# First layer of a two-layer network: the 64 left-over rows of its contraction as one full product of stacked high and low weights and two 64-row products on the two halves of the array

## The chip, the core and the metric

The kernel runs on one core of a Trainium2 chip. The metric is the device time of one execution in microseconds (us); the time before is the median of three runs. TensorE (PE) multiplies, VectorE (DVE) and ScalarE (ACT) read its results from the accumulator memory, GpSimd (POOL) works on ordinary memory only, and SyncE (SP) issues all transfers.

## The reference

```
S, D, DFF = 2048, 576, 4608
h  = x + irfft2(rfft2(layernorm(x)) * (w_r + i w_i))      # x: 2048 x 576
h2 = h + relu(layernorm(h) @ w1) @ w2                     # w1: 576 x 4608, w2: 4608 x 576
```

All of it is float32. The kernel keeps that precision in the two layers on products that take rounded inputs (type fp32r): each operand v is split into a high part (v rounded) and a low part (v minus the high part), and a product a·b becomes high·high + high·low + low·high, three products in place of one.

## The kernel before, in words

The work has four stages: the forward transform, a spectral stage (`mid_d`, `mid_b`, `mid_i`), the inverse transform mixed with the first units of the network, and the long part in which only the network is left, from about 225 us on.

**The units.** The hidden width of 4608 is cut into 18 groups of 256 (two halves of 128, index `a`), the 2048 tokens into 4 chunks of 512. A group with a chunk is a unit, 72 in all, in the order of the list `steps` (L685, L686). The first layer of a unit is `mm1` (L460 to L481): for each half, products of 512 columns that accumulate into one bank. The contraction over 576 is four full blocks of 128 rows and 64 left-over rows. Each full block takes three products (high weights with high tokens, high with low, low with high). For the left-over rows the tokens are stacked: block 4 of the token buffer `xc` holds the low part in partitions 0 to 63 and the high part in 64 to 127, and the high and low weights of block 4 stand twice, in both halves of the partitions. So one full product with the high weights gives high·low + high·high, and one with the low weights gives the rest (L470). That is 14 products a half and 28 a unit.

**The second layer.** The first 8 units multiply hidden values by `w2` in `mm2`. From unit 8 on (`WINO`), `slot` (L626) does it with seven products of half-size blocks, each of them six instructions of 288 columns (`prod`, L562), 42 a unit, whose results VectorE adds to the output (`add`, L569). The order is written out by hand: `quarter(k)` puts a quarter of the next unit's first layer between the products of this one, half `a = k // 2`, and the instructions whose number over 7 equals `k % 2`. The products of this unit and of the next share TensorE in that order, in two accumulators of the second layer (`wps[0]`, `wps[1]`) and two of the first (`wps[2]`, `wps[3]`, one for each half, used in turn by even and odd units).

**The weights.** `load_weights` loads a group's weights; the 64 left-over rows of `w1` are loaded twice, into both halves of the partitions (L300, L301). `split_weights` allots the high and low copies (five blocks of 256 columns) and lists the pieces. `split` (L305) makes the high part on ScalarE and the low part on VectorE (L307). From group 3 on `slot` does one piece at a time.

**The tokens.** In the inverse stage, `norm2` normalises two token tiles of 128 on ScalarE (`ln_apply`, L222), one at the end of each step of the loop at L689. `project` (L442 to L455) transposes a tile on TensorE in five blocks: four of columns 0 to 511 (L446) and a fifth of columns 448 to 575 (L447), which puts the left-over columns into partitions 64 to 127. ScalarE writes the high parts of all five blocks (L451) and a copy (L453), GpSimd subtracts for the low parts of the four full blocks (L454), VectorE for the left-over ones (L455, on 64 partitions). The token buffer has 9 blocks: 5 high ones and 4 low ones. At step 17 of the loop `project` comes before the products of the network (L703), otherwise behind them.

**Shapes of products.** In the spectral stage the products have 64 output rows; pairs of them go to output partitions 0 to 63 and 64 to 127 of the same bank (L336 to L341). All other products are full, 128 by 128. Float32 inputs make two instructions of a product, fp32r inputs one. `warm_pe` (L276) runs products of the identity that nobody reads; two calls (L386, L388) stand at the end of the spectral stage, behind 64-row outputs.

Of the kernel before, what the change touches and what calls it, by code (L numbers as in the profile page):

```python
# [11 lines left out]
F32R = mybir.dt.float32r  # L12
# [4 lines left out]
S, D, DFF = 2048, 576, 4608  # L17
# [110 lines left out]
def kernel(ctx: ExitStack, tc: tile.TileContext, x, w_r, w_i, w1, w2, cc2, c1, fb, ib, c3, out):  # L128
    nc = tc.nc
# [3 lines left out]
    def sb(shape, tag, bufs=1, dt=F32):  # L133
        n[0] += 1
        return pool.tile(shape, dt, tag=tag, name=f"{tag}_{n[0]}", bufs=bufs)

    n = [0]

    def ps():
        n[0] += 1  # L140
        return psum.tile([128, 1024], F32, tag="d", name=f"d_{n[0]}", bufs=4)

    def ebuf(shape, dt=F32):
        e = sb([128, EW], "e", EB, dt)[:, :int(np.prod(shape[1:]))]
        return e.rearrange("p (a b) -> p a b", a=shape[1]) if len(shape) == 3 else e

    def mm(o, l, r, start, stop):
        nc.tensor.matmul(o, l, r, start=start, stop=stop)  # L148

    def act(o, i, **kw):  # L150
        nc.scalar.activation(o, i, AF.Copy, **kw)  # L151

    xs = sb([128, NT, D], "X")
# [7 lines left out]
    ident = sb([128, 128], "ident")  # L161
# [55 lines left out]
    def ln_apply(xs, t0, k, mvr, zs):  # L217

        r = mvr[2]
        for i in range(k):  # L220
            yield
            nc.scalar.activation(zs[i], xs[:, t0 + i, :], AF.Identity, bias=r[:, 2, i:i + 1], scale=r[:, 1, i:i + 1])  # L222
# [6 lines left out]
    stats, zin = {}, {}  # L229
# [64 lines left out]
    raw, wts = {}, {}  # L294
# [9 lines left out]

    def split(h, l, v):  # L305
        act(h, v)
        nc.vector.tensor_sub(l, v, h)  # L307

    pieces = []

    def work(k):
        for _ in range(k):
            split(*pieces.pop(0))

    def split_weights(g, part):
        if g == 1 and part == 0:
            h, l = tail[0][:, 4608:5888], tail[0][:, 5888:7168]
        else:
            h, l = (ebuf([128, (1280, 1152)[part]], F32R) for _ in range(2))
        h, l = (v.rearrange("p (a n) -> p a n", a=(5, 2)[part]) for v in (h, l))  # L320
        wts[g, part] = h, l
        for k in range((5, 2)[part]) if g >= 2 else [slice(None)]:
            pieces.append((h[:, k], l[:, k], raw[g][part][:, k]))
        if g <= 2:
            work(len(pieces))

    tail = []
# [61 lines left out]
    xs = sb([128, NT, D], "A")  # L389
# [2 lines left out]

    dev = c3t[:, :580].rearrange("p (a n) -> p a n", a=4)
    lpv = c3t[:, 580:].rearrange("p (a n) -> p a n", a=2)
    xc01 = sb([128, 2, 9, 512], "B", dt=F32R)
    xc2 = sb([128, 9, 512], "C", dt=F32R)
    xc = [xc01[:, 0], xc01[:, 1], xc2]
    Es = {}

    def inv_d(t):  # L400
        pd = ps()
        ut = [dims(U, 64 * (32 * b + 2 * t), [1, 128]) for b in range(5)]
        for r in range(2):
            o = pd[:, 512 * r:512 * r + 290]
            mm(o, ut[4], lpv[:, r], True, False)
            for h in range(2):
                mm(o[:, 145 * h:145 * h + 145], ut[2 * ((r + h) % 2) + r], dev[:, 2 * r + h], False, h == 1)
        ez = ebuf([128, 578 + D])
        pdv = pd.rearrange("p (r n) -> p r n", r=2)
        e0, e1 = ez[:, :289], ez[:, 289:578]  # L410
        R2 = [289, 2]
        pa_, pb_ = pdv[:, :, 0:145], pdv[:, :, 145:290]
        ea = dims(ez, 0, R2, [1, 145])
        act(ea, pa_)
        nc.vector.tensor_sub(dims(ez, 288, R2, [-1, 144]), ea[:, :, :144], pb_[:, :, :144])  # L415
        nc.vector.tensor_add(ea, ea, pb_)  # L416
        y = ez[:, 578:]
        nc.gpsimd.tensor_sub(dims(ez, 578 + 575, [-1, 287]), e0[:, 1:288], e1[:, 1:288])
        nc.vector.tensor_add(y[:, 0:289], e0, e1)  # L419
        Es[t] = y  # L420
# [11 lines left out]
    def stat2(t):  # L432
        t0 = t - t % 2
        stats[t0] = ln_stats(xs, t0, 2, t % 2, stats.get(t0))

    def norm2(t0, k):
        z = ebuf([128, 2, D])
        for i in range(k):
            Zs[t0 + i] = z[:, i, :]
        return ln_apply(xs, t0, k, stats.pop(t0), [z[:, i, :] for i in range(k)])  # L440

    def project(t):  # L442
        y = Zs.pop(t)
        pz = ps()
        for b in range(4):
            nc.tensor.transpose(pz[:, 128 * b:128 * b + 128], y[:, 128 * b:128 * b + 128], ident)  # L446
        nc.tensor.transpose(pz[:, 512:640], y[:, 448:576], ident)  # L447
        q = slice(128 * (t % CH), 128 * (t % CH) + 128)
        dst = xc[t // CH]
        pzv = pz.rearrange("p (a s) -> p a s", s=128)  # L450
        act(dst[:, 0:5, q], pzv[:, :5])  # L451
        zt = ebuf([128, 512])
        act(zt, pz[:, :512])  # L453
        nc.gpsimd.tensor_sub(dst[:, 5:9, q], zt.rearrange("p (a s) -> p a s", s=128), dst[:, 0:4, q])  # L454
        nc.vector.tensor_sub(dst[0:64, 4, q], pzv[64:128, 4], dst[64:128, 4, q])  # L455

    hid = {}
    pend = {}

    def mm1(i, a, part=None):  # L460
        g, c = steps[i]
        w1h, w1l = wts[g, 0]
        if a == 0 and not part:
            pend[i] = None if i >= WINO else ps()
        p = hid_p(i, a) if i >= WINO else pend[i][:, 512 * a:512 * a + 512]
        f = slice(128 * a, 128 * a + 128)
        ops = []
        for kt in range(4):
            ops += [(w1h, kt, kt), (w1h, kt, 5 + kt), (w1l, kt, kt)]
        ops += [(w1h, 4, 4), (w1l, 4, 4)]  # L470
        for n_, (w, kt, xk) in enumerate(ops):
            if part is None or n_ // 7 == part:
                mm(p, w[:, kt, f], xc[c][:, xk, :], n_ == 0, n_ == len(ops) - 1)
        if i >= WINO:
            return
        if a == GF - 1:
            p = pend.pop(i).rearrange("p (a s) -> p a s", a=GF)
            hh, hl = sb([128, GF, 512], "D", 4, F32R), sb([128, GF, 512], "D", 4, F32R)
            nc.scalar.activation(hh, p, AF.Relu)
            nc.vector.scalar_tensor_tensor(hl, p, 0.0, hh, op0=ALU.max, op1=ALU.subtract)  # L480
            hid[i] = (hh, hl)  # L481
# [21 lines left out]
    WINO = 8  # L503
    wps, fs = [], {}
    NAMES = ("B22", "T4", "B11", "B21", "T2", "T1", "T3")

    def wform(n):
        o = 6208 + 576 * NAMES.index(n)
        return tail[0][:, o:o + 288], tail[0][:, o + 288:o + 576]

    def wino_sums(g, *ns):
# [9 lines left out]
    def wino_w(*names):  # L521
        for n in names:
            split(*wform(n), fs[n])

    def wino_tiles():
        D1, D2, D3 = (sb([128, 4, 256], "D", 4, F32R) for _ in range(3))
        E1, E2 = ebuf([128, 4, 256]), ebuf([128, 4, 256])
        hs = tail[0][:, 5184:5696], tail[0][:, 5696:6208]
        fs.update(p0=E1[:, 0:2], p1=E1[:, 2:4], S1=E2[:, 0], S2=E2[:, 1], S3=E2[:, 2], S4=E2[:, 3], S12=E2[:, 0:2])
        fs.update(A11=(D1[:, 0], D1[:, 1]), A12=(D1[:, 2], D1[:, 3]), A22=(D2[:, 0], D2[:, 1]), S4f=(D2[:, 2], D2[:, 3]))  # L530
        fs.update(S12f=(D3[:, 0:2], D3[:, 2:4]), S1f=(D3[:, 0], D3[:, 2]), S2f=(D3[:, 1], D3[:, 3]))
        fs.update(S3f=(tail[0][:, 5696:5952], tail[0][:, 5952:6208]))

    def relu_split(f, p):
        h, l = f
# [3 lines left out]
    def hid_p(i, k):  # L539
        return wps[2 + k][:, 512 * (i % 2):512 * (i % 2) + 512]  # L540
# [85 lines left out]
    def slot(i):  # L626
# [4 lines left out]
        def quarter(k):  # L631
            mm1(i + 1, k // 2, k % 2)
            if k % 2:
                hid_a(i + 1, k // 2)
# [54 lines left out]
    for t in range(NT + 6):  # L689
        if t < NT:  # L690
            inv_d(t)
        if t % 2 == 1 and 5 <= t <= NT + 3:
            gen = norm2(t - 5, 2)
            next(gen)
        if 0 <= t - 3 < NT:
            stat2(t - 3)
        if 0 <= t - 1 < NT:
            inv_a(t - 1)
        if t == 15:
            load_weights(1)  # L700
            tail.append(sb([128, 10240], "X", dt=F32R))
            xc.append(tail[0][:, :4608].rearrange("p (a n) -> p a n", a=9))
        if t == 17:  # L703
            project(t - 6)
        if 10 <= t < 22:
            i, u = divmod(t - 10, 4)
            if u < 2:
                mm1(i, u)
            else:
                if i == 2:  # L710
                    mm1(3, u - 2)
                mm2(i, 2 * u - 4)
                mm2(i, 2 * u - 3)
        if 6 <= t and t != 17:
            project(t - 6)
        if t in (2, 4):
            split_weights(0, t // 2 - 1)
        if t in (18, 19):
            split_weights(1, t - 18)
        if gen:  # L720
            next(gen, None)
# [49 lines left out]
```

## Time and profile before

| | |
|---|---|
| device time, three runs | 1055.39, 1053.37, 1055.37 us; median 1055.37 |
| profiled execution | span 1053.3 us from first to last instruction; no device time of its own is given beside it |
| instructions | 17197 |
| mean granted TensorE clock | 0.994 |

The page describes one profiled execution. "Busy" of an engine is the union of its instructions' times. Products on TensorE are pipelined, so records overlap, and the end of a product is a model; starts are what to compare. PE stands for products, PEld for loads of weights (the operand that stays in the array). A row of a group reads: line, engine, operation, what it writes and reads, shape, count | busy us, mean ns | idle time of the engine before it and what ended it. A shape of a product such as 128*64 is that of its weights, rows by columns. A row of the timeline reads: start, length, engine, line, operation, count, and in brackets the idle time before it.

### The profile page before, as it was taken

The numbers are of one execution on the slowest core, as the hardware profiler recorded it, in microseconds if no ns is written. First come the engines' busy times: TensorE is split into PE (matmuls) and PEld (weight loads), VectorE is DVE, ScalarE is ACT, GpSimd is POOL, SyncE is SP. The second block draws the span as 40 slices with busy tenths as digits, with TensorE's granted clock in tenths as the row PEclk, the third lists the DMA queues.
The fourth block names the chain that finished last, engine by engine and source line by source line (L and its number), as shares of the span: only waits on it lengthen the run. The fifth ranks groups of instructions, "written<-read, shape, count | busy, mean of one in ns | idle before, by whom it ended". The sixth has DMA issues, their size and how long they took to land.

```text
span 1053.3 us, 17197 instructions
## 1 busy us (share of the span) xinstructions
PE 1036.2 (98%) x6560; PEld 928.0 (88%) x6560; DVE 750.3 (71%) x1409; ACT 389.9 (37%) x846; POOL 328.0 (31%) x439
## 2 busy tenths in 40 slices
PE   8999999999999999999999999999999999999997
PEld 8888778799999999999999999999999999999996
DVE  7587696543477777778777777778777777777775
ACT  4533243431133333334333333434333333434332
POOL 4300164311133424333333423333333323243322
PEclk9999999999999999999999999999999999999999
DMA  8931700011000011000000001000000001100024
GB/s 239 248 92 49 180 2 26 23 48 48 1 26 23 26 36 36 26 23 26 24 26 23 26 24 48 26 23 26 24 26 23 26 24 40 34 23 2 1 63 117
DMA packets 31105, 48.05 MB, mean 46 GB/s; under 512 B 2992, under 2 KB 22704, under 8 KB 31024
## 3 DMA queue, kind: packets, MB, share of 16 engines
q1 hardware_dynamic: 31024, 46.96, 16.5%
q8 instruction: 52, 0.85, 0.3%
q14 instruction: 29, 0.24, 0.1%
HBM read 42.23 MB, written 4.72 MB: 45 GB/s over the span
## 4 chain that ended last, share of the span: by engine, by line
PE 95%; DVE 3%; ACT 1%; issue 0%; POOL 0%; DVEq 0%; POOLq 0%; ACTq 0%
PE d L148 60%; PE d L562 33%; PE d L276 1%; PE d L446 1%; DVE A L569 0%; DVE A L428 0%; DVE e L307 0%; DVE e L416 0%; DVE e L415 0%; ACT e L222 0%; DVE e L419 0%; DVE e L360 0%; DVE e L359 0%; PE d L447 0%; DVE e L354 0%
## 5 line engine op out<-in xcount | busy, mean ns | idle before, releaser
L569 DVE TENSOR_TENSOR A<-A,d 128x576 f32<-128x576 f32 (+1 forms) x449 | 334.5, 746 | 52.6 <-PE d L562 52.5
L562 PE MATMUL d<-X,D 128*128 128x288 f32 x2304 | 345.8, 294 | 1.8 <-DVE A L569 1.7
L562 PEld LDWEIGHTS d<-X,D 128*128 128x128 f32 x2304 | 328.8, 188 | 17.3 <-issue 1.7
L148 PE MATMUL d<-B,e 128*128 128x512 f32 x952 | 238.3, 391 | 0.4 <-DVE A L428 0.4
L148 PEld LDWEIGHTS d<-B,e 128*128 128x128 f32 x952 | 172.0, 188 | 28.8 <-ACT e L151 0.8
L537 DVE SCALAR_TENSOR_TENSOR D<-d,D 128x256 fp32r<-128x256 f32 x190 | 80.7, 425 | 120.6 <-ACT D L536 120.6
L536 ACT ACTIVATE D<-d 128x256 fp32r<-128x256 f32 x190 | 72.6, 382 | 237.6 <-PE d L148 237.6
L551 POOL TENSOR_TENSOR e<-e 128x256 f32<-128x256 f32 x63 | 46.6, 739 | 349.8 <-ACT e L550 349.8
L148 PE MATMUL d<-C,e 128*128 128x512 f32 x476 | 119.1, 390 | 0.0
L148 PE MATMUL d<-X,e 128*128 128x512 f32 x476 | 118.7, 390 | 0.0
L151 ACT ACTIVATE X<-e 128x288 fp32r<-128x288 f32 (+2 forms) x177 | 70.2, 434 | 103.5 <-PE d L562 103.5
L307 DVE TENSOR_TENSOR D<-e,D 128x256 fp32r<-128x256 f32 (+1 forms) x128 | 92.6, 724 | 20.1 <-ACT D L151 20.1
L547 POOL TENSOR_TENSOR e<-e 128x256 f32<-128x256 f32 x64 | 47.5, 743 | 173.8 <-ACT e L546 170.5
L148 PEld LDWEIGHTS d<-X,e 128*128 128x128 f32 x476 | 86.0, 188 | 13.8
L148 PEld LDWEIGHTS d<-C,e 128*128 128x128 f32 x476 | 85.8, 188 | 13.7
L151 ACT ACTIVATE D<-e 128x256 fp32r<-128x256 f32 (+1 forms) x130 | 67.4, 519 | 75.3 <-POOL e L552 70.4
L307 DVE TENSOR_TENSOR X<-e,X 128x288 fp32r<-128x288 f32 (+2 forms) x176 | 82.8, 493 | 0.9 <-ACT X L151 0.9
L562 PEld LDWEIGHTS d<-X 128*128 128x128 f32 x384 | 58.0, 188 | 4.9
L562 PE MATMUL d<-X 128*128 128x288 f32 x384 | 61.3, 295 | 0.0
L148 PE MATMUL d<-e,D 128*128 128x288 f32 x384 | 55.3, 303 | 0.3 <-DVE D L480 0.3
L148 PEld LDWEIGHTS d<-e,D 128*128 128x128 f32 x384 | 53.7, 194 | 1.4 <-DVE D L480 0.6
L552 POOL TENSOR_TENSOR e<-e,e 128x256 f32<-128x256 f32 x63 | 49.7, 788 | 4.9
(85 smaller groups left out, 994.4 us busy)
## 6 DMA issues: line engine op xcount, KB each, us to landing
e<-in_B_w_dram SPq DMA_DIRECT2D x18, 576.0 KB, 3.8
e<-in_B_w_dram SPq DMA_DIRECT2D x18, 512.0 KB, 3.7
A<-in_A_x_dram SPq DMA_DIRECT2D x16, 288.0 KB, 8.2
out_dram<-A SPq DMA_DIRECT2D x30, 144.0 KB, 2.5
X<-in_A_x_dram SPq DMA_DIRECT2D x12, 288.0 KB, 7.4
e<-in_B_w_dram SPq DMA_DIRECT2D x36, 64.0 KB, 3.5
B<-in_A_w_r_dram SPq DMA_DIRECT2D x15, 144.5 KB, 7.3
B<-in_A_w_i_dram SPq DMA_DIRECT2D x15, 144.5 KB, 7.2
```

The costliest lines, as they stand in the source:

```text
L148: nc.tensor.matmul(o, l, r, start=start, stop=stop)
L151: nc.scalar.activation(o, i, AF.Copy, **kw)
L276: nc.tensor.transpose(wm[:, :128], ident, ident)
L307: nc.vector.tensor_sub(l, v, h)
L446: nc.tensor.transpose(pz[:, 128 * b:128 * b + 128], y[:, 128 * b:128 * b + 128], ident)
L536: nc.scalar.activation(h, p, AF.Relu)
L537: nc.vector.scalar_tensor_tensor(l, p, 0.0, h, op0=ALU.max, op1=ALU.subtract)
L547: nc.gpsimd.tensor_sub(fs["S3"], fs["p0"][:, 0], fs["p0"][:, 1])
L551: nc.gpsimd.tensor_add(fs["S1"], fs["p0"][:, 1], fs["p1"][:, 1])
L552: nc.gpsimd.tensor_sub(fs["S2"], fs["S1"], fs["p0"][:, 0])
L562: nc.tensor.matmul(P[:, tt], l[:, q], r, start=first and n_ == 0, stop=n_ == 2, skip_group_check=not first)
L569: nc.vector.tensor_add(xt, xt, P)
```

## The change

For the left-over rows the roles of weights and tokens in the stacking are exchanged.

- Tokens: `norm2` lets GpSimd copy columns 512 to 575 of a normalised tile behind its end, and the fifth transpose takes columns 512 to 639. So all 128 partitions hold the left-over columns, twice. Block 4 of `xc` is their high part in both halves, and a new block 9 their low part in both halves, on VectorE with 128 partitions.
- Weights: block 4 of the high buffer becomes a stack. In the columns of the first half (`a` = 0) partitions 0 to 63 are high and 64 to 127 low; in those of the second half it is the other way round. `split` does it, when it gets no low buffer, with two VectorE instructions of 64 partitions and 128 columns. The low buffer loses its fifth block.
- Products: one full product of block 4 for each half gives high·high + low·high. High weights by low tokens is one product of 64 rows for each half: partitions 0 to 63 for the first half, 64 to 127 for the second. Both are issued one after the other, at the end of the first half's products: the first closes the first half's bank, the second opens the second half's.
- Buffers: the token buffers have 10 blocks; places in the `X` buffer shift; the memory set aside for transfers that software describes is set to 4096 bytes.

A unit has 26 full products of 512 columns and two of 64 rows in place of 28 full ones.

```
 def split(h, l, v):
     act(h, v)
-    nc.vector.tensor_sub(l, v, h)
+    if l is None:
+        for k, f in ((slice(64, 128), slice(0, 128)), (slice(0, 64), slice(128, 256))):
+            nc.vector.tensor_sub(h[k, f], v[k, f], h[k, f])
+    else:
+        nc.vector.tensor_sub(l, v, h)
...
-        for k in range((5, 2)[part]) if g >= 2 else [slice(None)]:
+        for k in range((4, 2)[part]) if g >= 2 else [slice(0, (4, 2)[part])]:
             pieces.append((h[:, k], l[:, k], raw[g][part][:, k]))
+        if part == 0:
+            pieces.append((h[:, 4], None, raw[g][0][:, 4]))
...
-    xc01 = sb([128, 2, 9, 512], "B", dt=F32R)
-    xc2 = sb([128, 9, 512], "C", dt=F32R)
+    xc01 = sb([128, 2, 10, 512], "B", dt=F32R)
+    xc2 = sb([128, 10, 512], "C", dt=F32R)
...
 def norm2(t0, k):
-    z = ebuf([128, 2, D])
+    z = ebuf([128, 2, D + 64])
     for i in range(k):
         Zs[t0 + i] = z[:, i, :]
-    return ln_apply(xs, t0, k, stats.pop(t0), [z[:, i, :] for i in range(k)])
+    for i, _ in enumerate(ln_apply(xs, t0, k, stats.pop(t0), [z[:, i, :D] for i in range(k)])):
+        if i:
+            nc.gpsimd.tensor_copy(z[:, i - 1, D:], z[:, i - 1, 512:D])
+        yield
+    nc.gpsimd.tensor_copy(z[:, k - 1, D:], z[:, k - 1, 512:D])
 
 def project(t):
...
-    nc.tensor.transpose(pz[:, 512:640], y[:, 448:576], ident)
+    nc.tensor.transpose(pz[:, 512:640], y[:, 512:640], ident)
...
-    nc.vector.tensor_sub(dst[0:64, 4, q], pzv[64:128, 4], dst[64:128, 4, q])
+    nc.vector.tensor_sub(dst[:, 9, q], pzv[:, 4], dst[:, 4, q])
...
 def mm1(i, a, part=None):
...
-        p = hid_p(i, a) if i >= WINO else pend[i][:, 512 * a:512 * a + 512]
+        ps_ = [hid_p(i, k) if i >= WINO else pend[i][:, 512 * k:512 * k + 512] for k in range(2)]
...
-        ops += [(w1h, 4, 4), (w1l, 4, 4)]
+        ops += [(w1h, 4, 4)]
         for n_, (w, kt, xk) in enumerate(ops):
-            if part is None or n_ // 7 == part:
-                mm(p, w[:, kt, f], xc[c][:, xk, :], n_ == 0, n_ == len(ops) - 1)
+            if part is None or (n_ >= 7 - a) == part:
+                mm(ps_[a], w[:, kt, f], xc[c][:, xk, :], a == 0 and n_ == 0, a == 1 and n_ == 12)
+        if a == 0 and part != 0:
+            for k in range(2):
+                r = slice(64 * k, 64 * k + 64)
+                mm(ps_[k], w1h[r, 4, 128 * k:128 * k + 128], xc[c][r, 9, :], k == 1, k == 0)
...
-            tail.append(sb([128, 10240], "X", dt=F32R))
-            xc.append(tail[0][:, :4608].rearrange("p (a n) -> p a n", a=9))
+            tail.append(sb([128, 10752], "X", dt=F32R))
+            xc.append(tail[0][:, :5120].rearrange("p (a n) -> p a n", a=10))
...
-    nc = _bacc.Bacc("TRN2", target_bir_lowering=False, num_devices=1)
+    nc = _bacc.Bacc("TRN2", target_bir_lowering=False, num_devices=1, dynamic_dma_scratch_size=4096)
```

On TensorE, in a unit of the long part, from the second quarter (end of the first half) into the third. `X` is the token buffer, the two `e` buffers are the group's high and low weights (the one that stands first is high); the `d` of the first row is the first half's accumulator. Before:

```order
L148 MATMUL d_2579<-X_1872,e_7372 128x512
L148 MATMUL d_2579<-X_1872,e_7373 128x512
L148 MATMUL d_2579<-X_1872,e_7372 128x512 x2
L148 MATMUL d_2579<-X_1872,e_7373 128x512
L148 MATMUL d_2579<-X_1872,e_7372 128x512
L148 MATMUL d_2579<-X_1872,e_7373 128x512
L562 MATMUL d_2688<-X_1872,D_2583 128x288 x6
L562 MATMUL d_2689<-X_1872,D_2583 128x288 x6
L148 MATMUL d_2580<-X_1872,e_7372 128x512 x2
L148 MATMUL d_2580<-X_1872,e_7373 128x512
L148 MATMUL d_2580<-X_1872,e_7372 128x512 x2
L148 MATMUL d_2580<-X_1872,e_7373 128x512
```

The same place in the changed kernel, where `prod` is at L576:

```order
L148 MATMUL d_2602<-X_1886,e_7406 128x512
L148 MATMUL d_2602<-X_1886,e_7407 128x512
L148 MATMUL d_2602<-X_1886,e_7406 128x512 x2
L148 MATMUL d_2602<-X_1886,e_7407 128x512
L148 MATMUL d_2602<-X_1886,e_7406 128x512 x2
L148 MATMUL d_2603<-X_1886,e_7406 128x512
L576 MATMUL d_2711<-X_1886,D_2606 128x288 x6
L576 MATMUL d_2712<-X_1886,D_2606 128x288 x6
L148 MATMUL d_2603<-X_1886,e_7406 128x512 x2
L148 MATMUL d_2603<-X_1886,e_7407 128x512
L148 MATMUL d_2603<-X_1886,e_7406 128x512 x2
L148 MATMUL d_2603<-X_1886,e_7407 128x512
```

The last product with low weights is gone; the second of the "x2" before the narrow products and the row behind it are the two 64-row products (their rows show the output, which has 128 partitions), the second into the other half's accumulator. The third quarter has one full product less before the next narrow ones.

On GpSimd, in the inverse stage, about the tiles 9 to 12: `L454` and, after, `L464` is the subtraction in `project`; `L418` and `L424` belong to the inverse transform, the lines from `L211` to `L214` to the statistics. Before:

```order
L454 TENSOR_TENSOR C_1286<-e_1837,C_1286 128x4x128
L418 TENSOR_TENSOR e_1849<-e_1849 128x287
L454 TENSOR_TENSOR C_1286<-e_1898,C_1286 128x4x128
L211 TENSOR_SCALAR r_1858<-mv_1857 128x2
L212 TENSOR_TENSOR r_1858<-r_1858,half_141 128x2
L214 TENSOR_SCALAR r_1858<-mv_1857,r_1858 128x1 x2
L454 TENSOR_TENSOR C_1286<-e_1949,C_1286 128x4x128
```

After:

```order
L464 TENSOR_TENSOR C_1286<-e_1850,C_1286 128x4x128
L450 COPY e_1751<-e_1751 128x64
L424 TENSOR_TENSOR e_1863<-e_1863 128x287
L464 TENSOR_TENSOR C_1286<-e_1911,C_1286 128x4x128
L448 COPY e_1869<-e_1869 128x64
L211 TENSOR_SCALAR r_1872<-mv_1871 128x2
L212 TENSOR_TENSOR r_1872<-r_1872,half_141 128x2
L214 TENSOR_SCALAR r_1872<-mv_1871,r_1872 128x1 x2
L464 TENSOR_TENSOR C_1286<-e_1963,C_1286 128x4x128
```

Behind each subtraction stands a copy of the next tile's 64 columns (`L448`, `L450`).

More of the change, by code (lines that the diff above doesn't have):

```diff
@@ L316, in split_weights @@
         if g == 1 and part == 0:
-            h, l = tail[0][:, 4608:5888], tail[0][:, 5888:7168]
+            h, l = tail[0][:, 5120:6400], tail[0][:, 6400:7424]
         else:
-            h, l = (ebuf([128, (1280, 1152)[part]], F32R) for _ in range(2))
-        h, l = (v.rearrange("p (a n) -> p a n", a=(5, 2)[part]) for v in (h, l))
+            h, l = (ebuf([128, n], F32R) for n in ((1280, 1024), (1152, 1152))[part])
+        h, l = (v.rearrange("p (a n) -> p a n", n=(256, D)[part]) for v in (h, l))
         wts[g, part] = h, l
-        for k in range((5, 2)[part]) if g >= 2 else [slice(None)]:
+        for k in range((4, 2)[part]) if g >= 2 else [slice(0, (4, 2)[part])]:
             pieces.append((h[:, k], l[:, k], raw[g][part][:, k]))
+        if part == 0:
+            pieces.append((h[:, 4], None, raw[g][0][:, 4]))
         if g <= 2:
@@ L507, in wform @@
     def wform(n):
-        o = 6208 + 576 * NAMES.index(n)
+        o = 6720 + 576 * NAMES.index(n)
         return tail[0][:, o:o + 288], tail[0][:, o + 288:o + 576]
@@ L527, in wino_tiles @@
         E1, E2 = ebuf([128, 4, 256]), ebuf([128, 4, 256])
-        hs = tail[0][:, 5184:5696], tail[0][:, 5696:6208]
+        hs = tail[0][:, 5696:6208], tail[0][:, 6208:6720]
         fs.update(p0=E1[:, 0:2], p1=E1[:, 2:4], S1=E2[:, 0], S2=E2[:, 1], S3=E2[:, 2], S4=E2[:, 3], S12=E2[:, 0:2])
@@ L531, in wino_tiles @@
         fs.update(S12f=(D3[:, 0:2], D3[:, 2:4]), S1f=(D3[:, 0], D3[:, 2]), S2f=(D3[:, 1], D3[:, 3]))
-        fs.update(S3f=(tail[0][:, 5696:5952], tail[0][:, 5952:6208]))
+        fs.update(S3f=(tail[0][:, 6208:6464], tail[0][:, 6464:6720]))
     def relu_split(f, p):
```

## The prediction

> **What bounds the kernel now.** I read the page first: shares of busy time, the slices of TensorE and its clock, and the chain that ended last.
>
> ```profile
> PE 1036.2 (98%) x6560; PEld 928.0 (88%) x6560; DVE 750.3 (71%) x1409; ACT 389.9 (37%) x846; POOL 328.0 (31%) x439
> PE   8999999999999999999999999999999999999997
> PEclk9999999999999999999999999999999999999999
> PE 95%; DVE 3%; ACT 1%; issue 0%; POOL 0%; DVEq 0%; POOLq 0%; ACTq 0%
> ```
>
> TensorE is busy in every slice at full clock, and 95% of the chain is its own work. A busy TensorE can still hide waits, so I looked next at what it waits for, in the groups by line and shape (busy, mean ns | idle before), and at busy time in a stretch of the long steady part:
>
> ```profile
> L562 PE MATMUL d<-X,D 128*128 128x288 f32 x2304 | 345.8, 294 | 1.8 <-DVE A L569 1.7
> L148 PE MATMUL d<-B,e 128*128 128x512 f32 x952 | 238.3, 391 | 0.4 <-DVE A L428 0.4
> L148 PE MATMUL d<-C,e 128*128 128x512 f32 x476 | 119.1, 390 | 0.0
> 500.00:600.00 100.00, 100.00 (x588) 90.62 (x587) 75.86 (x136) 38.68 (x94) 33.15 (x41) 1.00 0.08 26
> ```
>
> The two large kinds, 288 columns wide (second layer) and 512 wide (first layer), wait 1.8 and 0.4 us in the whole run. VectorE has 24% of the stretch free, the others more. So the time is the sum of TensorE's products, and a product less is worth what it occupies in the stream. The mean of 391 ns isn't that: products are pipelined and overlap in the records. The spacing is read from the timeline of TensorE (start, length, group, count):
>
> ```profile
> 599.85 1.75 PE L562 MATMUL d<-X,D 128*128 128x288 f32 x12
> 601.44 1.75 PE L148 MATMUL d<-X,e 128*128 128x512 f32 x7
> 603.03 1.75 PE L562 MATMUL d<-X,D 128*128 128x288 f32 x12
> 604.61 1.75 PE L148 MATMUL d<-X,e 128*128 128x512 f32 x7
> ```
>
> Seven wide products take 603.03 - 601.44 = 1.59 us from start to start, 0.227 us each; twelve narrow ones also 1.59 us, 0.132 each. A unit (one weight group with one chunk of 512 tokens; 18 groups x 4 chunks = 72 units) has 28 wide and 42 narrow products: 28 x 0.227 + 42 x 0.132 = 11.9 us.
>
> **The change part by part: the products.** For the 64 left-over rows a unit now runs four full wide products (for each half, high weights by the stacked high and low tokens, then low weights by the same). After, it runs two full ones and two of 64 rows each. Per unit two full products go: 2 x 0.227 = 0.454 us, 32.7 us over 72 units. The two that come cost one product time if they run side by side on the two halves of the array, and two if not.
>
> The trace of before has no product of 64 rows. The nearest it has is products of 64 columns (spectral stage, L148, d<-e,A), whose neighbours go to different halves of the output partitions. The full products of L401 to L407 (d<-e,X) have the same widths:
>
> ```profile
> 88.44 2.14 PE L148 MATMUL d<-e,A 128*64 128x290 f32 x24
> 90.42 1.14 PE L148 MATMUL d<-e,C 128*64 128x289 f32 x8
> 104.64 0.42 PE L148 MATMUL d<-e,A 128*64 128x290 f32 x2
> 149.48 2.13 PE L148 MATMUL d<-e,X 128*128 128x290 f32 x12
> 151.45 1.22 PE L148 MATMUL d<-e,cc 128*128 128x288 f32 x4
> ```
>
> 24 half-array products take 90.42 - 88.44 = 1.98 us; 12 full ones of the same widths take 151.45 - 149.48 = 1.97. A pair (third row) is over within 0.42 us though one alone is given 0.41: the partner starts 0.01 behind. So halves do run side by side here, and I take the same for halves by rows: a pair costs 0.227 + 0.01. Without anything else the products give 72 x (0.454 - 0.237) = 15.6 us back.
>
> **The switches.** The pair of a unit stands between full products: TensorE goes from full to 64-row products and back, 144 times. What such a change costs can be seen where the spectral stage ends in full products of the identity (L276), twice:
>
> ```profile
> 111.65 0.23 PE L148 MATMUL d<-D,e 128*64 128x64 f32 x2
> 111.97 0.38 PE L276 MATMUL d<-ident 128*128 128x128 f32 x2
> 114.86 0.28 PE L148 MATMUL d<-D,e 128*64 128x64 f32 x4
> 114.91 0.23 PE L148 MATMUL d<-D,e 128*64 128x64 f32 x2
> 115.07 0.33 PE L276 MATMUL d<-ident 128*128 128x128 f32 x1
> 115.24 0.38 PE L276 MATMUL d<-ident 128*128 128x128 f32 x2
> 115.35 0.38 PE L276 MATMUL d<-ident 128*128 128x128 f32 x2
> 115.07 1.29 PEld L276 LDWEIGHTS d<-ident 128*128 128x128 f32 x12
> ```
>
> The last pairs come 0.05 apart (114.86, 114.91), full ones of the identity 0.11 apart (115.24, 115.35). Unbroken, the second full product would have started 0.05 + 0.11 = 0.16 after the last pair. It started 0.33 after it (114.91 to 115.24), and 0.32 the other time (111.65 to 111.97). So 0.16 us is lost: about 0.10 until the first weights are loaded (the last row begins at 115.07, no waited-for engine in brackets), and 0.06 because these are loaded in the open (that product lasts 0.33, not the 0.27 of its followers).
>
> I take 0.16 for each of the 144 switches: the nearest row, though of halves by columns, and of leaving the halves only; entering them is always behind a wait for another engine there. The ends are 0 (row halves need no pause) and 0.22 (another 0.06 of open loading): 0 to 31.7 us, and 144 x 0.16 = 23.0. The number of weight loads stays at 70 a unit.
>
> The rule that speaks against the change stands in the Trainium skill, TensorEngine Tiling (Array Packing), section Key Properties: going to another tile within a mode is free, while changing the mode drains TensorE, and 64x128 is a mode of its own there. Of the rule the rows above show the one case they hold. TensorE: Matmul & The Clock Gate (the Trainium skill), section Single matmul latency, gives a constant of 166 ns for a warm product beyond its columns; with that per switch my estimate would be 144 x 0.166 = 23.9 us instead of 23.0.
>
> **What else moves.** The fifth transpose of a token tile (L447) now reads a copy of columns 512 to 575 that GpSimd makes, queued behind its subtraction of the tile before (L454). It matters where the transposes follow the normalisation at once, as for tile 11:
>
> ```profile
> 196.93 0.87 ACT L222 ACTIVATE e<-A,r 128x576 f32<-128x576 f32 x1
> 197.12 1.27 POOL L454 TENSOR_TENSOR C<-e,C 128x512 fp32r<-128x512 f32 x1 [1.68 <-ACT e L151]
> 197.84 0.66 PE L446 MATMUL d<-ident,e 128*128 128x128 f32 x4 [2.04 <-ACT e L222]
> 198.34 0.27 PE L447 MATMUL d<-ident,e 128*128 128x128 f32 x1
> L259 POOL COPY e<-e 128x4 f32<-128x4 f32 x6 | 1.2, 193 | 3.4 <-DVE e L254 3.4
> L547 POOL TENSOR_TENSOR e<-e 128x256 f32<-128x256 f32 x64 | 47.5, 743 | 173.8 <-ACT e L546 170.5 <-DVE A L569 3.2
> ```
>
> The copy can start at 197.12 + 1.27 = 198.39 and lasts between 0.19 and 0.74 (the last two rows: a tiny copy, and a subtraction four times as wide); I take 0.35, as it is narrow. The transpose moves from 198.34 to 198.74: 0.4 us (ends 0.2 to 0.8). For the other 15 tiles a whole step of TensorE's work lies between normalisation and transposes, or GpSimd is free when it ends, so I put those at nothing; uncovered, each would cost up to 0.35.
>
> VectorE splits the fifth weight block with two instructions on 64 partitions instead of one on 128, once in each of 18 groups:
>
> ```profile
> L307 DVE TENSOR_TENSOR e<-e,e 128x256 fp32r<-128x256 f32 x80 | 34.0, 429 | 0.0
> L455 DVE TENSOR_TENSOR C<-d,C 64x128 fp32r<-64x128 f32 x4 | 1.2, 293 | 4.8 <-ACT e L151 4.8
> ```
>
> That is 2 x 0.293 - 0.429 = 0.16 us a group, 2.8 in all, hidden under the 24% that VectorE has free; with that cover gone, at most 2.8. L455 itself works on 128 partitions instead of 64, on the same 128 columns. The pair opens the second half's accumulator one quarter earlier; it was last read two units before, so nobody waits. ScalarE's work and the transfers keep their sizes, and no transfer is moved past another. Buffer sizes change nothing in the order.
>
> **Sum.** -15.6 + 23.0 + 0.4 = +7.8 us. The profiled span is 1053.3 us; the page gives no device time of that execution beside it, and the runs took 1053.37 to 1055.39, so some 0.1 to 2.1 us lie around it. All terms lie inside the span; 1061.1 of span, or 1055.4 + 7.8 = **1063.2 us** against the median.
>
> **Rivals.**
> 1. *Row halves need no pause* (faster). The switch rows are of column halves only; in a row pair all 128 output columns stay in use. Against it: weights and products of two shapes meet in the same array, and column halves paid both times. -15.6 + 0.4: 1040.2 us. Chance 0.24.
> 2. *Only one of the two directions pays* (faster). Leaving is what the trace shows, entering isn't seen. -15.6 + 72 x 0.16 + 0.4 = -3.7: 1051.7 us. Chance 0.12.
> 3. *The pause is there, the weights are loaded during it* (no change): 0.10 per switch. -15.6 + 14.4 + 0.4 = -0.8: 1054.6 us. Against it: both times the load came after the pause. Chance 0.08.
> 4. *The change doesn't do what it says*: the 64-row products run one after the other. Column pairs speak against it. Without switches the wide products of a unit would again take 28 times, 1055.8 us, chance 0.03; with switches 1055.8 + 23.0 = 1078.8 us, chance 0.05.
>
> The point from which the sign turns: a switch of 15.2 / 144 = 0.106 us. VectorE becoming the bound is no rival: even by rival 1 its share rises only from 75.9% to 77%.
>
> **How the numbers follow.** The forecast, both directions paying about 0.16, has chance 0.48, time 1063.2. Its own range: below, one of the two loads covered (72 x 0.06 = 4.3 less), 1058.9; above, one load more in the open (4.3 more), 1067.5. A measurement of this kernel can tell about 0.2%, 2.1 us, from no change. Faster: rivals 1 and 2, 0.36. Within 0.2%: rival 3 and the first half of 4, 0.11. Slower: the forecast and the second half of 4, 0.53. Leaving out rival 1 would leave out 0.24 and more, so the range reaches to it, with about a microsecond below for its GpSimd term and stagger: 1039 to 1067.5. Only the last case of rival 4 lies outside.
>
> **What would show it.** In the profile after: rows of L148 with 64*128, 144 of them. From the first wide product of the quarter that holds the pair to the next narrow one: now 7 x 0.227 = 1.59 us; by the forecast 6 x 0.227 + 0.237 + 0.32 = 1.92; by rival 1, 1.60; by rival 2, 1.76. The quarter after it has six products, 1.36 instead of 1.59. The weight load behind a pair should start after a gap, and the full product behind it last longer than 391 ns. A unit takes 12.0 us by the forecast and 11.7 by rival 1. Two starts of a pair a whole product apart would mean that the halves don't run side by side. The forecast is wrong if the quarter with the pair takes under 1.8 us.

## The result and the profile after

The changed kernel takes 1072.16 us (median of four runs, 1071.51 to 1073.46) beside 1055.38 for the kernel before: ratio of the runs 1.0169, 95% interval 1.0155 to 1.0183 (the two medians alone give 1.0159). It is slower, as forecast, but by 16.8 us instead of 7.8, and outside the range. Runs of one kernel differ by 2 to 3 us, the longer ones mostly at a lower granted clock (the kernel before, on one chip: 1053.3 to 1053.5 us at 0.998 or more, 1054.9 at 0.996). Ratios below are against the kernel before on the same chip.

The page's rows for the engines, TensorE's clock and the chain:

```profile
PE 1049.9 (98%) x6560; PEld 908.6 (85%) x6560; DVE 760.0 (71%) x1429; ACT 390.0 (36%) x848; POOL 331.2 (31%) x455
PEclk9999999999999999999999999999999999999999
PE 95%; DVE 2%; POOL 1%; ACT 1%; issue 0%; DVEq 0%; POOLq 0%; ACTq 0%
```

TensorE is as busy as before and its clock as full. Loads of weights (PEld) are as many, yet busy for 19.4 us less; most of that (72 x 0.18) is the two loads of a pair lying on top of each other. And GpSimd (POOL) has come into the chain.

The unit's length is read off one group that runs once a unit: the six narrow products that read only `X`. Two of its rows in the timeline, before and after:

```profile
606.20 0.96 PE L562 MATMUL d<-X 128*128 128x288 f32 x6
618.11 0.96 PE L562 MATMUL d<-X 128*128 128x288 f32 x6
```

```profile
604.20 0.96 PE L576 MATMUL d<-X 128*128 128x288 f32 x6
616.30 0.96 PE L576 MATMUL d<-X 128*128 128x288 f32 x6
```

11.91 us have become 12.10. 72 x 0.19 = 13.7 us of the 17.0 by which the span grew (1053.3 to 1070.3, both at a mean granted clock of 0.994). Inside a unit, the quarter with the pair (x8: six full products and two halves), the narrow products behind it and the next quarter:

```profile
599.25 1.96 PE L148 MATMUL d<-C,e 128*128 128x512 f32 x8
601.13 1.85 PE L576 MATMUL d<-X,D 128*128 128x288 f32 x12
602.82 1.54 PE L148 MATMUL d<-C,e 128*128 128x512 f32 x6
604.20 0.96 PE L576 MATMUL d<-X 128*128 128x288 f32 x6
```

The quarter takes 601.13 - 599.25 = 1.88 us, near the 1.92 of the forecast. The twelve narrow products behind it take 1.69 instead of 1.59; the forecast had counted all of the way back into the quarter. The next quarter takes 1.38, as said (1.36). How the pair itself is framed, from narrow windows of the timeline on TensorE's products and loads:

```profile
600.16 0.61 PE L148 MATMUL d<-C,e 128*128 128x512 f32 x2
600.70 0.50 PE L148 MATMUL d<-C,e 64*128 64x512 f32 x2
600.70 0.18 PEld L148 LDWEIGHTS d<-C,e 64*128 64x128 f32 x2 [0.35 <-issue]
601.13 0.57 PEld L576 LDWEIGHTS d<-X,D 128*128 128x128 f32 x4 [0.25 <-issue]
601.13 0.54 PE L576 MATMUL d<-X,D 128*128 128x288 f32 x2
```

The last full product starts at 600.16 + 0.61 - 0.39 = 600.38 (a full one is recorded with 0.39). Unbroken, its follower would start at 600.61; the pair's loads start at 600.70, 0.09 later, having waited for no engine ("issue"). Then the pair is recorded with 0.50 us, not 0.39: 0.11 of loading in the open. Both halves start within 0.01 of each other, so they run side by side. Behind them the loads wait again (0.25 <-issue) until 601.13, that is 0.43 after the pair's start: 0.11 of loading, 0.23 of product, 0.09 of pause. The next two products cover 0.54 instead of 0.43: 0.11 of loading once more. So a switch costs 0.09 + 0.11 = 0.20 us, both ways.

### The profile page after: what moved, and what is told of

Read it like the earlier page. It is cut to its first block, busy times and chain, and to the rows that moved or that the text cites. A ratio compares the mean times of both kernels' runs of the same rounds, so it can differ in the third digit from the quotient of the medians.

```text
span 1070.3 us, 17256 instructions
## 1 busy us (share of the span) xinstructions
PE 1049.9 (98%) x6560; PEld 908.6 (85%) x6560; DVE 760.0 (71%) x1429; ACT 390.0 (36%) x848; POOL 331.2 (31%) x455
## 4 chain that ended last, share of the span: by engine, by line
PE 95%; DVE 2%; POOL 1%; ACT 1%; issue 0%; DVEq 0%; POOLq 0%; ACTq 0%
PE d L148 59%; PE d L576 34%; PE d L276 1%; PE d L456 0%; DVE A L583 0%; POOL B L464 0%; POOL r L212 0%; PE d L457 0%; ACT e L151 0%; ACT e L222 0%; DVE e L422 0%; DVE e L425 0%; DVE e L366 0%; DVE e L421 0%; DVE e L365 0%
## 5 line engine op out<-in xcount | busy, mean ns | idle before, releaser
L576 PE MATMUL d<-X,D 128*128 128x288 f32 x2304 | 352.7, 297 | 1.8 <-DVE A L583 1.7
L576 PEld LDWEIGHTS d<-X,D 128*128 128x128 f32 x2304 | 324.0, 188 | 27.8 <-issue 17.2
L148 PE MATMUL d<-B,e 128*128 128x512 f32 (+1 forms) x952 | 238.2, 399 | 0.0
L148 PEld LDWEIGHTS d<-B,e 128*128 128x128 f32 (+1 forms) x952 | 165.5, 188 | 37.9 <-issue 11.5
L311 DVE TENSOR_TENSOR D<-e,D 128x256 fp32r<-128x256 f32 (+1 forms) x128 | 92.3, 721 | 9.0 <-ACT D L151 1.2
L148 PEld LDWEIGHTS d<-X,e 128*128 128x128 f32 x476 | 82.6, 188 | 18.8 <-issue 6.2
L148 PEld LDWEIGHTS d<-C,e 128*128 128x128 f32 x476 | 82.6, 188 | 18.6 <-issue 6.0
L311 DVE TENSOR_TENSOR X<-e,X 128x288 fp32r<-128x288 f32 (+2 forms) x176 | 82.8, 493 | 0.7 <-ACT X L151 0.7
L576 PEld LDWEIGHTS d<-X 128*128 128x128 f32 x384 | 58.1, 188 | 4.9
L576 PE MATMUL d<-X 128*128 128x288 f32 x384 | 61.4, 295 | 0.0
```

The lines of the kernel that those rows point to most:

```text
L576: nc.tensor.matmul(P[:, tt], l[:, q], r, start=first and n_ == 0, stop=n_ == 2, skip_group_check=not first)
```

## The experiments

**Full products instead of the pair.** In `mm1`, at the same place:

```
         if a == 0 and part != 0:
             for k in range(2):
-                r = slice(64 * k, 64 * k + 64)
-                mm(ps_[k], w1h[r, 4, 128 * k:128 * k + 128], xc[c][r, 9, :], k == 1, k == 0)
+                mm(ps_[k], w1h[:, 4, 128 * k:128 * k + 128], xc[c][:, 9, :], k == 1, k == 0)
```

> The two 64-row products of a unit become two full products at the same place (the stacked weights of each half by the low tokens of all 128 partitions, which adds low by low); the rest is as in the changed kernel. Switch theory: a pair occupies 0.63 us of TensorE (0.227 side by side and two switches of 0.20), two full products 0.454, so 72 x 0.176 = 12.7 us less than the changed kernel: 1059.5 us, and no pause in the records at that place. Rival, the loss comes from the place and not from the shape (the second half's bank opened a quarter earlier, the weights split in two): pauses stay, 1072 us.

Measured: 1058.71 us, ratio 1.0050 (1.0033 to 1.0066). The unit, and the waits of the narrow products:

```profile
609.35 0.96 PE L575 MATMUL d<-X 128*128 128x288 f32 x6
621.26 0.96 PE L575 MATMUL d<-X 128*128 128x288 f32 x6
L575 PE MATMUL d<-X,D 128*128 128x288 f32 x2304 | 345.8, 294 | 1.8 <-DVE A L582 1.7
```

11.91 us, the unit of before to the hundredth, and the narrow products are busy for the same 345.8 us. The place, the early opening of the second bank and the split weights cost nothing in the unit; the shape of the two products does. All the rest of the change costs 3.2 us by the spans (1056.5 and 1053.3). It falls before unit 8, where the first such group starts 3.1 us later than in the kernel before (first row):

```profile
296.45 0.96 PE L562 MATMUL d<-X 128*128 128x288 f32 x6
299.54 0.96 PE L575 MATMUL d<-X 128*128 128x288 f32 x6
```

The ratio says more, 5.3 us (0.0050 x 1053.5; 3.5 to 7.0 by its interval). What makes up the difference of the two was not settled.

**No pair at all.** The loop of the pair goes, and the banks are opened and closed by full products.

```
...
-        if a == 0 and part != 0:
-            for k in range(2):
-                r = slice(64 * k, 64 * k + 64)
-                mm(ps_[k], w1h[r, 4, 128 * k:128 * k + 128], xc[c][r, 9, :], k == 1, k == 0)
```

> Leaves out the product of high weights by low tokens for the left-over rows: 26 full products a unit and no 64-row ones. Switch theory: all 0.63 us of a pair go, 72 x 0.63 = 45.4 us less than the changed kernel: 1026.8 us. Rival, a pair costs only its product time of 0.227 and the loss is elsewhere: 72 x 0.227 = 16.3 us less, 1055.8 us.

Measured: 1026.68 us, ratio 0.9741 (0.9719 to 0.9764).

```profile
606.82 0.96 PE L572 MATMUL d<-X 128*128 128x288 f32 x6
618.28 0.96 PE L572 MATMUL d<-X 128*128 128x288 f32 x6
```

A unit takes 11.46 us. The two full products of the run above are worth 0.45, as the spacing said; the pair is worth 12.10 - 11.46 = 0.64, of which 0.23 is product and 0.41 the stay in 64-row shape: 0.21 for each of two switches.

**One half of the pair.** The second half's 64-row product is left out; a full product opens the second half's bank.

```
...
-            for k in range(2):
-                r = slice(64 * k, 64 * k + 64)
-                mm(ps_[k], w1h[r, 4, 128 * k:128 * k + 128], xc[c][r, 9, :], k == 1, k == 0)
+            mm(ps_[0], w1h[0:64, 4, 0:128], xc[c][0:64, 9, :], False, True)
```

> Keeps the 64-row product of the first half only, so that of the second half is left out; both switches of a unit stay. Switch theory with halves side by side: the second half costs only its late start, 72 x 0.004 = 0.3 us, so 1072 us as in the changed kernel. Rival, the halves run one after the other and the switches are small (0.09 each): one product time a unit goes, 16.3 us, 1056 us.

Measured: 1070.3 us, ratio 1.0155 (1.0135 to 1.0176).

```profile
598.62 0.50 PE L148 MATMUL d<-C,e 64*128 64x512 f32 x1
602.11 0.96 PE L574 MATMUL d<-X 128*128 128x288 f32 x6
614.20 0.96 PE L574 MATMUL d<-X 128*128 128x288 f32 x6
```

12.09 us, 0.01 less than with both, and the one half is recorded with the same 0.50 us as the pair. The second half is nearly free, so the rival that the halves run one after the other falls.

**The pair twice.** The pair's loop runs two times in a row.

> Each unit's pair of 64-row products is issued twice in a row (so high weights by low tokens counts double): four 64-row products, still one stay in 64-row shape. If the pause belongs to the change of shape, the second pair costs its product time alone, 72 x 0.23 = 16.6 us more than the changed kernel: 1089 us, a unit 12.33 us. Rival, every 64-row product pays for itself (a load in the open, a pause): 72 x 0.65 = 46.8 us more, 1119 us, a unit 12.75.

Measured: 1090.46 us, ratio 1.0344 (1.0325 to 1.0363).

```profile
599.17 0.96 PE L577 MATMUL d<-X 128*128 128x288 f32 x6
606.32 2.19 PE L148 MATMUL d<-C,e 128*128 128x512 f32 x10
608.43 1.89 PE L577 MATMUL d<-X,D 128*128 128x288 f32 x12
610.16 1.54 PE L148 MATMUL d<-C,e 128*128 128x512 f32 x6
611.54 0.96 PE L577 MATMUL d<-X 128*128 128x288 f32 x6
```

12.37 us: a second pair costs 0.27 where it follows the first, not 0.64. The expectation had 12.33. The quarter with the pairs takes 608.43 - 606.32 = 2.11 us, 0.23 more than with one pair (1.88). That is one product time, with no pause between the pairs. The other 0.04 lies in the narrow products behind (1.73 instead of 1.69); its cause is open.

**The halves parted.** Each half's 64-row product stands at the end of its own half's products; every half's bank is opened by a full product.

```
...
-        if a == 0 and part != 0:
-            for k in range(2):
-                r = slice(64 * k, 64 * k + 64)
-                mm(ps_[k], w1h[r, 4, 128 * k:128 * k + 128], xc[c][r, 9, :], k == 1, k == 0)
+        if part != 0:
+            r = slice(64 * a, 64 * a + 64)
+            mm(ps_[a], w1h[r, 4, f], xc[c][r, 9, :], False, True)
```

> The two 64-row products of a unit are parted: the first half's stays at the end of the first half's products, the second half's comes at the end of the second half's. The products are the same, but there are two stays in 64-row shape a unit. If a stay costs 0.42 us beyond its products: 72 x (0.42 + 0.23) = 46.8 us more than the changed kernel, 1119 us, a unit 12.75 us. Rival, the halves never ran side by side and the pauses are small (0.09 each): 72 x 0.19 = 13.4 us more, 1085.6 us.

Measured: 1113.34 us, ratio 1.0561 (1.0542 to 1.0580). The unit, and one half product with what follows it:

```profile
598.20 0.96 PE L575 MATMUL d<-X 128*128 128x288 f32 x6
605.96 1.95 PE L148 MATMUL d<-B,e 128*128 128x512 f32 x7
607.85 1.85 PE L575 MATMUL d<-X,D 128*128 128x288 f32 x12
610.91 0.96 PE L575 MATMUL d<-X 128*128 128x288 f32 x6
```

12.71 us: the same products as in the changed kernel cost 0.61 us more because they make two stays. The forecast was 0.65 and 1119 us; the time came out 5.7 us lower, and 72 x 0.04 = 2.9 of that is the unit. Six full products and a half take 1.89 us here; before, seven full ones took 1.59.

**The copy on ScalarE.** In `norm2`, the copy of 64 columns becomes a second activation from the same input.

```
-                nc.gpsimd.tensor_copy(z[:, i - 1, D:], z[:, i - 1, 512:D])
...
+            for o, src in ((slice(0, D), slice(0, D)), (slice(D, D + 64), slice(512, D))):
+                nc.scalar.activation(z[:, i, o], xs[:, t0 + i, src], AF.Identity, bias=r[:, 2, i:i + 1], scale=r[:, 1, i:i + 1])
```

> The copy of the 64 left-over columns is made by a second activation on ScalarE from the same input, not by GpSimd; the products are those of the changed kernel. If GpSimd's copy costs the two waits of 2.03 and 1.48 us that the trace shows before the fifth transpose of tiles 1 and 3: 3.5 us less, less 0.3 for the added activations, 1069.0 us. Rival, the prediction's 0.4 us holds and those waits are made up for later: 1071.8 us.

Measured: 1069.3 us, ratio 1.0141 (1.0126 to 1.0157). The ratio's interval overlaps that of the changed kernel; the trace decides. The fifth transpose, in the changed kernel and in this one:

```profile
L457 PE MATMUL d<-ident,e 128*128 128x128 f32 x16 | 4.6, 288 | 3.6 <-POOL e L450 3.5
```

```profile
L457 PE MATMUL d<-ident,e 128*128 128x128 f32 x16 | 4.5, 282 | 0.0
L450 ACT ACTIVATE e<-A,r 128x64 f32<-128x64 f32 x16 | 7.0, 435 | 0.0
```

The waits of 3.6 us are gone and the span is 1067.5 instead of 1070.3, 2.8 less. The unit is unchanged. So GpSimd's copy costs about 2.8 us more than the same copy on ScalarE, and not 0.4.

**One stay for two units.** From unit 8 on the pairs of two neighbouring units of a group stand together; the first 8 units use full products as in the first experiment, and the copy is on ScalarE.

```
...
+            elif c % 2 == 0:
+                for u in range(2):
+                    for k in range(2):
+                        r = slice(64 * k, 64 * k + 64)
+                        mm(hid_p(i + u, k), w1h[r, 4, 128 * k:128 * k + 128], xc[c + u][r, 9, :], u + k > 0, u + k == 0)
```

> From unit 8 on, the pairs of two neighbouring units of a group stand together (four 64-row products, one stay for two units; the second unit's banks are opened by them); the first 8 units use full products instead of the pair; the copy of the left-over columns is on ScalarE. A unit without its pair takes 11.46 us by the run without one; two pairs and a stay add 0.46 + 0.42 for two units, so 11.90 us a unit against 11.91 before: 64 x 0.013 = 0.8 us less than before, 0.3 us more for the copies. Switch theory: within 0.2% of the kernel before, ratio 0.9995. Rival, the pause grows with what is opened or loaded in a stay: a unit at 12.1 us, 12 us more than before, ratio 1.011.

Measured: 1054.67 us, ratio 1.0008 (0.9999 to 1.0017).

```profile
593.35 0.96 PE L582 MATMUL d<-X 128*128 128x288 f32 x6
604.81 0.96 PE L582 MATMUL d<-X 128*128 128x288 f32 x6
617.18 0.96 PE L582 MATMUL d<-X 128*128 128x288 f32 x6
```

A unit without a stay takes 11.46 us (604.81 - 593.35), one with both pairs 12.37, 11.915 on average against 11.91 before: the gain of the side-by-side halves pays one stay in two units, and no more. The forecast ratio of 0.9995 lies just outside the interval: it had 11.90 us a unit, with 0.23 for the second pair where the doubled pair above cost 0.27. Halving the stays brings the kernel back to the time of before, not below it. One stay for four units would need eight banks for the first layer alone, more than it has (four); it wasn't tried.

## Why the prediction was right in kind and wrong in size

- **What bounds the kernel** held. TensorE's stream sets the time, and a full product is worth 0.227 us: two of them 0.45 in the run without a pair.
- **Halves side by side** held: half a pair less saves 0.01 us a unit.
- **The switch, in both directions,** held as the mechanism, and rivals 1 to 4 fall: the loads stop for no engine on both sides of a pair, and two stays cost twice. The rule of the Trainium skill (TensorEngine Tiling (Array Packing), Key Properties) that a change of mode drains TensorE, and one of tile alone doesn't, agrees with the rows: there is a pause on both sides of a pair, and none inside the doubled pair. The price is in the rows alone, 0.20 us, and the prediction's second estimate of a switch, 0.166 us, was short of it too.
- **The size of the switch** is the first step that failed: 0.16 forecast, 0.21 measured, 144 x 0.05 = 7 us. The pause was right (0.10, measured 0.09); the open load was not (0.06, measured 0.11). The prediction took it from products of the identity, whose loads are shorter than those of fp32r weights. The trace of before held the right row, a narrow product behind a wait for ScalarE near the end; beside it, the identity's loads:

```profile
1041.52 0.30 PEld L562 LDWEIGHTS d<-X,D 128*128 128x128 f32 x2 [0.64 <-ACT D L151]
115.07 0.20 PEld L276 LDWEIGHTS d<-ident 128*128 128x128 f32 x2
```

The records of the two loads of a row overlap; I take the start of the second as the moment when the first was in place. Loads are recorded with 0.19 us in the first row and 0.14 in the second, so the first load took 0.30 - 0.19 = 0.11 of an fp32r block, and 0.20 - 0.14 = 0.06 of the identity. The 0.11 is what the rows around the pair show. The Trainium skill, TensorE: Matmul & The Clock Gate, section LDWEIGHTS, gives the number of columns over 1.2 as the nanoseconds of a load, by which I estimate 107 ns for 128 columns: the fp32r loads agree, the identity's don't. What makes the identity's shorter wasn't tried.
- **GpSimd's copy** is the second: 0.4 forecast, about 2.8 measured. The prediction looked at tile 11 and put the others at nothing because GpSimd would be free. It wasn't, for tiles 1 and 3: their copies queue behind a subtraction that is late itself, as the trace of before shows for tile 1.

```profile
141.60 0.27 PE L447 MATMUL d<-ident,e 128*128 128x128 f32 x1
142.05 1.28 POOL L454 TENSOR_TENSOR B<-e,B 128x512 fp32r<-128x512 f32 x1
```

The transpose that now waits for the copy ran at 141.60, and the subtraction ahead of the copy began only at 142.05. In the changed kernel the wait stands there in full, and again for tile 3 (last row):

```profile
142.30 1.26 POOL L464 TENSOR_TENSOR B<-e,B 128x512 fp32r<-128x512 f32 x1
143.51 0.47 POOL L450 COPY e<-e 128x64 f32<-128x64 f32 x1
144.03 0.33 PE L457 MATMUL d<-ident,e 128*128 128x128 f32 x1 [2.03 <-POOL e L450]
152.71 0.33 PE L457 MATMUL d<-ident,e 128*128 128x128 f32 x1 [1.48 <-POOL e L450]
```

For tile 11, which the prediction did look at, the fifth transpose starts 0.78 us behind the first of the four (before: 198.34 - 197.84 = 0.50), 0.28 more where 0.40 was forecast:

```profile
200.70 0.66 PE L456 MATMUL d<-ident,e 128*128 128x128 f32 x4 [2.04 <-ACT e L222]
201.48 0.34 PE L457 MATMUL d<-ident,e 128*128 128x128 f32 x1
```

- **VectorE, the transfers and the buffers** cost nothing in the unit, as said: with full products it is that of before. Outside it, what the rest of the change costs beyond the copy is 3.2 - 2.8 = 0.4 us by the spans, and 5.3 - 2.8 = 2.5 by the ratio; its cause is open.
- **The range** failed by its own terms. The text gave 0.22 as the upper end of a switch, but let only one of a unit's two switches reach it. With both at 0.22, and the copy at its own end of 0.8, -15.6 + 31.7 + 0.8 gives 1072.3 us, which takes in the measured time. The sum with the measured sizes: -15.6 + 144 x 0.21 + 2.8 = 17.4 us against 16.8 measured.

## What to carry to other kernels

In this kernel a single pair of products over half the rows of the array was not worth its place: the two halves together cost one product, but going there and back cost 0.41 us, more than the 0.23 that was saved. Two pairs in a stay came out even, so by these numbers a stay has to be shared by more than two before it pays; no run had more. The price of a load in the open must be read from a load of the same type and shape, behind any wait that shows it. And an instruction put on an engine "with time to spare" must be followed in that engine's queue for every tile, first of all where the queue starts up.

## What the runs showed of the hardware that was not expected

- Both directions of the switch cost the same, 0.09 us of pause and 0.11 of open loading; two 64-row loads into the two halves of the array take the open time of one (the pair is recorded with 0.50, as is the single half).
- GpSimd's sixteen copies of 128 x 64 took 0.23 to 0.25 us twelve times, 0.47 or 0.48 three times and 0.82 once. The four long ones, those of tiles 1 and 3 among them, ran beside a VectorE instruction that reads both its inputs from ordinary memory (L425, first row, beside the copy at 143.51; or L311); none of the short ones did. That this is what slows them is not shown: no run changed it.

```profile
142.32 1.56 DVE L425 TENSOR_TENSOR e<-e 128x289 f32<-128x289 f32 x1
189.42 0.24 POOL L450 COPY e<-e 128x64 f32<-128x64 f32 x1
```
